# First stage of a spectral filter and bilinear GLU kernel by pairs of row tiles

## The chip, the cores and the metric

The kernel runs on one core of a Trainium2 chip. The metric is device time in microseconds (us) for one execution. Engines are named as in the profile: PE is the matrix engine and PEld its weight loads, DVE the vector engine, ACT the scalar (activation) engine, POOL the GpSimd engine, SP the queue that issues most transfers. Each engine takes its own instructions strictly in program order and waits on semaphores for the others.

## The reference

Two residual layers on an array of 2048 rows and 640 columns, all float32. The change touches only the beginning of the first one.

```python
x = A_x                                            # [1, 2048, 640]
X = rfft2(layernorm(x)) * (w_r + 1j * w_i)         # [2048, 321] spectrum
h = x + irfft2(X, s=(2048, 640))
g, u = layernorm(h) @ w_gate, layernorm(h) @ w_up  # 640 -> 1728
out = h + (g * u) @ w_down                         # 1728 -> 640
```

Layer norm has no weights: each row is shifted by its mean and scaled by the inverse root of its variance plus 1e-5.

## The kernel before

The 2048 rows lie in 16 row tiles of 128. The Fourier transforms are done as matrix products with tables.

**The first stage** (lines 255 to 298) treats one row tile `t` at a time and leaves a partial transform in the array `s1`. What follows, from line 300 on, needs all 16 tiles of `s1`, so the next stage's first matrix product (the helper at line 82, reading `tab` and `s1`) can't begin before tile 15 is in `s1`. For a tile the engines do this:

- Statistics. For tiles 1, 4, 5 and 10 to 15, ACT makes two passes over the row with an accumulated sum (lines 149 and 150, in `moments`; the written rows go to a scratch part of `fold` and aren't used). For the others DVE uses its batch-norm instructions (134 to 136). Tiles form groups for the next step: (0), (1), (2,3), (4,5), (6 to 9), (10 to 13), (14,15). `inverse_root` then needs a square root on ACT (159, result `sd`) and four short DVE steps: a reciprocal (160), then 161, 162 and 163. The work of a group is spread over earlier tiles by the lists `dve` and `acts`. The root of a group goes to `post`, called in the iteration two tiles ahead of the group's first tile; the four DVE steps go to the iteration after it.
- Fold. The row is folded about its middle. POOL writes the differences (`odd`, line 183), DVE writes the sums less twice the mean (193), and then DVE adds the ends of the folded halves (the small sums `j`, 66 numbers a row, line 197) and subtracts them (320 numbers a row, line 198).
- Table. `scale_c` multiplies a constant 128x128 table by the row's inverse root (line 217 on DVE, or 215 on ACT for tile 0), so that the layer norm's scale enters by the matrix product.
- Product. `s1_mm`: six matrix instructions with the folds (line 209). The first four read the folded halves, the last two read `j`; so two thirds can run before lines 197 and 198 are done, the rest not. A seventh (line 210) reads `j` too and goes to a bank of its own. A float32 product counts as two passes in the profile: 12 for line 209 and 2 for line 210.
- Evacuation. ACT copies the tile's result to `s1`: `s1_main` (228, 512 numbers a row) and `s1_rest` (223, 128 numbers a row).

`fold` has four buffers, so tile `t` takes the place of tile `t - 4`. The tables `crs` have four places too. The main result bank has two buffers; the bank for the last product has one for even and one for odd tiles.

What sets the order is the loop at line 265: the order of calls is the order in each engine's queue. In iteration `t` ACT gets `s1_rest(t - 1)`, the statistics of `acts[t]`, the root in `post[t]` and `s1_main(t - 1)`; DVE gets the three fold steps of tile `t`, zipped with the short steps of `dve[t]`, and then the table of tile `t + 1`.

Of the kernel before, what the change touches and what calls it, by code (L numbers as in the profile page):

```python
# [11 lines left out]
F32 = mybir.dt.float32  # L12
F32R = mybir.dt.float32r
AF = mybir.ActivationFunctionType
OP = mybir.AluOpType

P = 128
S, D, NF, FF = 2048, 640, 321, 1728
NT = S // P
# [2 lines left out]
NC = 14  # L22
FW = (160, 193, 161, 161)
FOFF = (0, 160, 353, 514)
NR = 4
ON_ACT = (1, 4, 10, 14)
EPS = 1e-5

# [1 line left out]
def view(t, offset, dims):  # L30
    return bass.AP(tensor=t.tensor, offset=t.offset + offset, ap=[list(t.ap[0])] + [list(d) for d in dims])
# [6 lines left out]
def zipped(main, side):  # L38
    n = len(main)
    for i, f in enumerate(main):  # L40
        f()
        for h in side[i * len(side) // n:(i + 1) * len(side) // n]:
            h()
# [3 lines left out]
def tile_spectral_glu(ctx: ExitStack, tc: tile.TileContext, x, wf, wgu, wlast, wdown, wdlast,  # L47
                      cc, ci, fmain, frem, imain, irem, mm, out):
    nc = tc.nc
# [3 lines left out]
    small = ctx.enter_context(tc.tile_pool(name="small", bufs=4))  # L53
    ctx.enter_context(tc.manual_schedule())

    tt, act = nc.vector.tensor_tensor, nc.scalar.activation
# [9 lines left out]
    def bank(tag, bufs=2):  # L66
        return pools["a"].tile([P, 512], F32, tag=tag, name=tag, bufs=bufs)
# [31 lines left out]
    def home(tag, shape, name, dt=F32):  # L99
        return keep.tile(shape, dt, tag=tag, name=name)  # L100
# [10 lines left out]
    s1r = home("wA", [P, 2, NG, P], "s1r", F32R)  # L111
    fold = home("qm", [P, NR * 1026 + 2 * D], "fold")
    wts = home("wB", [P, 3, 2, 2, NQ], "wts")
# [10 lines left out]
    def moments(ts, junk=None, total=None):  # L124
        n = len(ts)
        m2 = small.tile([P, n], F32, tag="m2", name="m2")
        ve = small.tile([P, n], F32, tag="ve", name="ve")
        if junk is None:
            mv = small.tile([P, n, 2], F32, tag="mv", name="mv")

            def one(t, i):
                st = small.tile([P, 2, 6], F32, tag="st", name="st")
                return [
                    lambda: nc.vector.bn_stats(st[:, 0], X[t][:, 0:320]),
                    lambda: nc.vector.bn_stats(st[:, 1], X[t][:, 320:640]),
                    lambda: nc.vector.bn_aggr(mv[:, i], st),
                ]

            fs = [f for i, t in enumerate(ts) for f in one(t, i)]
            fs.append(lambda: nc.vector.tensor_scalar(m2, mv[:, :, 0], 2.0, None, op0=OP.mult))  # L140
            fs.append(lambda: nc.vector.tensor_scalar(ve, mv[:, :, 1], EPS, None, op0=OP.add))
            return m2, ve, fs
        sq = small.tile([P, n], F32, tag="sq", name="sq")
        fs = []
        if total is not None:
            fs.append(lambda: nc.vector.tensor_scalar(m2, total, 2.0 / D, None, op0=OP.mult))
        for i, t in enumerate(ts):
            if total is None:
                fs.append(lambda t=t, i=i: act(junk[i], X[t], AF.Identity, scale=2.0 / D, accum_out=m2[:, i:i + 1]))  # L149
            fs.append(lambda t=t, i=i: act(junk[i], X[t], AF.Square, bias=m2[:, i:i + 1], scale=-2.0,  # L150
                                           accum_out=sq[:, i:i + 1]))
        fs.append(lambda: nc.vector.tensor_scalar(ve, sq, 0.25 / D, EPS, op0=OP.mult, op1=OP.add))
        return m2, ve, fs
# [14 lines left out]
    def front(ts):  # L168
        n = len(ts)
        r = small.tile([P, n], F32, tag="r", name="r")  # L170
        junk = [fold[:, o:o + D] for o in (NR * 1026, NR * 1026 + D)]
        m2, ve, fs = moments(ts, junk * 2 if ts[0] in ON_ACT else None)
# [4 lines left out]
    def folded(t):  # L177
        o = t % NR * 1026
        return fold[:, o:o + 642], fold[:, o + 642:o + 1026]

    def odd(t):
        f = folded(t)[0]
        nc.gpsimd.tensor_tensor(view(f, 0, [[160, 2], [1, 160]]), view(XP[t], 1, [[320, 2], [1, 160]]),
                                view(XP[t], 639, [[-320, 2], [-1, 160]]), op=OP.subtract)

    def even(t):
        f, j = folded(t)

        def both(n):
            return view(f, 0, [[320, 2], [1, n]]), view(f, 160, [[321, 2], [1, n]])  # L190

        return [
            lambda: nc.vector.scalar_tensor_tensor(view(f, 320, [[161, 2], [1, 161]]),
                                                   view(XP[t], 0, [[320, 2], [1, 161]]), SC[t][1],
                                                   view(XP[t], 640, [[-320, 2], [-1, 161]]),
                                                   op0=OP.subtract, op1=OP.add),
            lambda: tt(view(j, 33, [[-33, 2], [1, 33]]), *both(33), op=OP.add),
            lambda: tt(view(j, 64, [[1, 2], [2, 160]]), *both(160), op=OP.subtract),
        ]

    PS1, CR = {}, {}

    def s1_mm(t):
        pm, pr = PS1[t] = bank("im"), bank("ir2" if t % 2 else "im2", 1)
        (f, j), c = folded(t), CR[t]
        sums = [(f[:, o:o + P], f[:, o + n:o + n + P]) for o, n in ((31, 160), (353, 161))]
        for k, ls in enumerate((*sums, (view(j, 128, [[2, P]]),), (view(j, 129, [[2, P]]),))):
            for n, l in enumerate(ls):
                nc.tensor.matmul(pm[:, k * P:(k + 1) * P], l, c, start=n == 0, stop=n == len(ls) - 1)  # L209
        nc.tensor.matmul(pr[:, 0:P], j[:, 0:P], c, start=True, stop=True)  # L210

    def scale_c(t):
        CR[t] = crs[t % 4]
        if t == 0:
            act(CR[t], cct, AF.Copy, scale=SC[t][0])
        else:
            nc.vector.tensor_scalar(CR[t], cct, SC[t][0], None, op0=OP.mult)

    def at(base, t):
        return view(base, 4 * t, [[64, 32], [1, 4]])  # L220

    def s1_rest(t):
        act(at(s1[:, 4], t), PS1[t][1][:, 0:P].rearrange("p (g m) -> p g m", g=32), AF.Copy)

    def s1_main(t):
        n = 4 if t < NT - 1 else 2
        for c in range(0, 4, n):
            act(view(s1, 4 * t + 2048 * c, [[2048, n], [64, 32], [1, 4]]),
                PS1[t][0][:, c * P:(c + n) * P].rearrange("p (c g m) -> p c g m", c=n, g=32), AF.Copy)
# [6 lines left out]
    dve = [[] for _ in range(NT)]  # L236
    acts = [[] for _ in range(NT)]
    post = {}
# [23 lines left out]
        post[first - 2] = cs[0]  # L262
        dve[first - 1] += cs[1:]
    odd(0)
    for t in range(NT):
        if t == 1:
            nc.gpsimd.dma_start(frt, frem)
        if t >= 1:
            s1_rest(t - 1)
            for f in acts[t]:  # L270
                f()
        if t:
            zipped(even(t), dve[t])
        else:
            e0 = even(0)
            for f in e0[:1] + c0 + e0[1:] + f1:
                f()
        if t >= 1:
            if t in post:
                post[t]()  # L280
            s1_main(t - 1)
        else:
            scale_c(0)
            for f in c1[:1] + acts[0]:
                f()
            zipped(dve[0], c1[1:])
        if t + 1 < NT:
            if t < 2:
                nc.gpsimd.tensor_copy(small.tile([P, 1], F32, tag="hold", name="hold"), folded(t)[1][:, 383:384])
            odd(t + 1)  # L290
            scale_c(t + 1)
        if t == 0:
            post[t]()
        s1_mm(t)
    s1_main(NT - 1)
    s1_rest(NT - 1)
    part(0, nc.vector)
# [743 lines left out]
    for n, (blk, p) in enumerate(steps):  # L1041
        if p == 6:
            s13, s12 = count % 3, (count + 1) % 3
            if blk == 0:
                load_raw(0)
                copies, sums, high, low = prep(0, blk, nc.vector)
# [24 lines left out]
            else:  # L1071
                copies, sums, high, low = prep(0, blk)
# [222 lines left out]
```

## Time and profile before

| what | value |
|---|---|
| median of 3 runs | 707.47 us (707.27 to 707.54) |
| the profiled execution's own time | 707.21 us |
| its span, first to last instruction | 705.2 us |
| what lies around the span | 2.0 us |
| busy share of the span: PE, PEld, DVE, ACT, POOL | 97%, 85%, 68%, 43%, 53% |
| granted clock of PE | 0.999 |
| first stage: first product of tile 0 to last `s1_main` | 8.46 us to 45.82 us |

Shares over the whole span mix stages with different limits. The first stage is 37 us of 705, and there DVE is the busy engine while PE has gaps; after it PE is nearly always busy. So what the change is worth has to be read from the first 46 us alone. In the rows of the timeline the first two numbers are the start and the duration in us, and the bracket at the end holds the idle time before the row and what ended it. Consecutive instructions of a kind are merged into one row (x12).

### The profile page before, as it was taken

How to read it: one execution, taken by the hardware profiler on the slowest of the kernel's cores; microseconds unless marked ns; L12 is line 12 of the kernel's file. 1: busy time of each engine (PE TensorE's matmuls, PEld its weight loads, DVE VectorE, ACT ScalarE, POOL GpSimd, SP SyncE). 2: the span in 40 equal slices, each digit the busy share in tenths (PEclk: the TensorE clock that was granted, in tenths of full speed). 3: DMA queues.
4: the chain of work that ended last, by engine and by line, in shares of the span. 5: the costliest groups of instructions: out<-in, count | busy, mean ns of one | idle time of the engine just before them, and what ended most of it. 6: DMA issues, size and time to landing. Idle time of an engine off the chain costs nothing.

```text
span 705.2 us, 10146 instructions
## 1 busy us (share of the span) xinstructions
PE 685.1 (97%) x3784; PEld 602.7 (85%) x3784; DVE 476.1 (68%) x830; ACT 305.3 (43%) x586; POOL 374.4 (53%) x355
## 2 busy tenths in 40 slices
PE   7899998999989999999999999999999999999998
PEld 6798997977878898988888889888888988888887
DVE  7968887798968445656565659555665656565654
ACT  4856776355543323242523355353333342424320
POOL 3312224332144586877868643148596877867610
PEclk9999999999999999999999999999999999999999
DMA  9405665002321211203020262311211103030203
GB/s 335 182 8 194 224 212 173 1 19 94 113 76 37 75 39 34 78 1 113 0 86 28 94 221 97 132 38 37 76 38 45 68 5 109 0 105 9 74 1 150
DMA packets 23233, 60.30 MB, mean 86 GB/s; under 512 B 2576, under 2 KB 7184, under 8 KB 23184
## 3 DMA queue, kind: packets, MB, share of 16 engines
q1 hardware_dynamic: 22608, 57.94, 23.9%
q0 software_dynamic: 288, 1.48, 0.6%
q8 instruction: 30, 0.49, 0.3%
q10 hardware_dynamic: 288, 0.23, 0.1%
q14 instruction: 19, 0.16, 0.1%
HBM read 51.78 MB, written 7.86 MB: 85 GB/s over the span
## 4 chain that ended last, share of the span: by engine, by line
PE 81%; DVE 10%; issue 5%; ACT 3%; DMA 1%; POOL 0%; SPq 0%; DVEq 0%; POOLq 0%; ACTq 0%
PE e L82 43%; PE y L82 25%; PE re L82 2%; PE im L82 2%; PE u L342 2%; PE eo L82 2%; PE im L209 1%; DVE ex L752 1%; PE im L392 1%; PE im L391 1%; PE ir L383 1%; DMA raw<-in_wgu_dram 1%; DVE x L515 1%; ACT fold L149 1%; DMA x<-in_x_dram 1%
## 5 line engine op out<-in xcount | busy, mean ns | idle before, releaser
L82 PE MATMUL e<-xt,wst 128*128 128x512 f32 x864 | 219.0, 392 | 1.7 <-ACT u L661 1.7
L82 PEld LDWEIGHTS e<-xt,wst 128*128 128x128 f32 x864 | 158.0, 188 | 29.1 <-ACT u L661 2.1
L82 PE MATMUL y<-wd,ht 128*128 128x320 f32 x880 | 150.8, 310 | 1.3 <-DVE x L513 1.0
L82 PEld LDWEIGHTS y<-wd,ht 128*128 128x128 f32 x880 | 138.7, 188 | 13.1 <-DVE x L513 1.3
L716 POOL TENSOR_TENSOR wst<-raw,wst 128x1024 fp32r<-128x1024 f32 x24 | 57.7, 2403 | 91.2 <-ACT wst L715 91.1
L82 PE MATMUL e<-t,wst 128*128 128x512 f32 x288 | 74.1, 391 | 0.0
L732 POOL TENSOR_TENSOR wst<-raw,wst 128x896 fp32r<-128x896 f32 (+1 forms) x46 | 65.1, 1438 | 8.0 <-ACT wst L727 8.0
L926 DVE TENSOR_TENSOR xb<-y,xb 128x640 f32<-128x640 f32 x60 | 49.5, 824 | 26.0 <-PE y L82 24.5
L748 ACT ACTIVATE ht<-e 128x512 fp32r<-128x512 f32 x48 | 27.6, 596 | 88.2 <-DVE rawh L844 44.4
L82 PEld LDWEIGHTS e<-t,wst 128*128 128x128 f32 x288 | 52.6, 188 | 8.5
L926 DVE TENSOR_TENSOR x<-y,x 128x640 f32<-128x640 f32 x48 | 39.5, 824 | 20.8 <-PE y L82 19.3
L1011 DVE TENSOR_TENSOR m<-e,m 128x512 f32<-128x512 f32 x24 | 16.5, 687 | 46.5 <-PE e L82 46.4
L752 DVE TENSOR_TENSOR ht<-e,ht 128x512 fp32r<-128x512 f32 x48 | 33.1, 689 | 17.6 <-ACT ht L748 17.0
L727 ACT ACTIVATE wst<-raw 128x896 fp32r<-128x896 f32 (+1 forms) x48 | 30.1, 677 | 31.5 <-POOL raw L721 30.7
L82 PE MATMUL y<-ex,ht 128*128 128x320 f32 x216 | 43.5, 309 | 0.0
L469 POOL TENSOR_TENSOR wd<-draw,wd 128x640 fp32r<-128x640 f32 x10 | 16.4, 1660 | 50.0 <-ACT wd L468 50.0
L82 PE MATMUL e<-xt,wdir 128*128 128x512 f32 x180 | 42.1, 393 | 0.0
L82 PEld LDWEIGHTS e<-xt,wdir 128*128 128x128 f32 x180 | 33.5, 188 | 7.2 <-issue 0.2
L82 PEld LDWEIGHTS y<-ex,ht 128*128 128x128 f32 x216 | 36.2, 188 | 3.1
L882 ACT ACTIVATE wd<-draw 128x640 fp32r<-128x640 f32 x18 | 13.3, 740 | 58.7 <-POOL draw L895 48.1
L82 PE MATMUL e<-ht,wst 128*128 128x512 f32 x144 | 38.4, 392 | 0.0
L513 DVE TENSOR_TENSOR x<-y,x 128x640 f32<-128x640 f32 x32 | 26.2, 819 | 17.7 <-PE y L82 17.7
(214 smaller groups left out, 1293.4 us busy)
## 6 DMA issues: line engine op xcount, KB each, us to landing
raw<-in_wgu_dram SPq DMA_DIRECT2D x24, 640.0 KB, 4.0
wts<-in_wf_dram SPq DMA_DIRECT2D x16, 644.0 KB, 4.3
draw<-in_wdown_dram SPq DMA_DIRECT2D x24, 320.0 KB, 4.5
x<-in_x_dram SPq DMA_DIRECT2D x16, 320.5 KB, 6.1
bits<-in_mm_dram SPq DMA_DIRECT2D x32, 128.0 KB, 3.9
sp<-x SPq DMA_DIRECT2D x8, 320.0 KB, 2.2
xb<-sp SPq DMA_DIRECT2D x8, 320.0 KB, 5.7
out_dram<-x SPq DMA_DIRECT2D x8, 320.0 KB, 2.3
```

Source lines behind the costliest of these rows:

```text
L82: nc.tensor.matmul(o, l, r, start=start, stop=stop, skip_group_check=True)
L342: nc.tensor.matmul(ps[h][:, 0:NQ], WM[g][0][:, h], T[g][:, h], start=True, stop=True)
L469: los.append(lambda r=r, a=a, b=b: engine.tensor_tensor(w[:, 1, a:b], r, f32(w[:, 0, a:b]), op=OP.subtract))
L513: tt(xv, ps[:, :, 0:320], xv, op=OP.add)
L716: nc.gpsimd.tensor_tensor(wa[:, 1], stage[:, 0:1024], f32(wa[:, 0]), op=OP.subtract)
L727: act(ws[:, 0, o:o + b - a], stage[:, a:b], AF.Copy)
L732: ptt(ws[:, 1, o:o + b - a], stage[:, a:b], f32(ws[:, 0, o:o + b - a]), op=OP.subtract)
L748: act(unit(u)[0], src, AF.Copy)
L752: engine.tensor_tensor(lo, src, f32(hi), op=OP.subtract)
L882: act(w[:, 0, a:b], r, AF.Copy)
L926: tt(xv, PQ[q][:, :, 0:320], xv, op=OP.add)
L1011: tt(m5, acc_a, m5, op=OP.add)
```

## The change

From tile 2 on, tiles are taken in pairs `(t, t + 1)`.

- The sums less twice the mean stay one DVE instruction a tile (`sum_fold`, now line 202). The small sums of both tiles become one DVE instruction (line 196), and so do the differences (line 197). They therefore come after the sums of both tiles.
- `fold` has six buffers instead of four.
- The tables of tiles 4 to 15 are made by ACT (line 221) instead of DVE (line 223).
- The loop is written anew. At the head of the iteration of a pair, ACT gets `s1_main` and `s1_rest` of both tiles of the pair before; then `acts[t]`, `post[t]`, `acts[t + 1]` and the tables of the next pair.
- Tiles 0 and 1 keep their order, except that `s1_main(0)` follows at once on tile 1's fold and `odd(3)` and `scale_c(3)` come ahead of pair (2,3).

Later lines have moved: 193 is 202, 197 is 196, 198 is 197, 209 is 215, 210 is 216, 217 is 223, 215 is 221, 223 is 229, 228 is 234. Lines 134 to 183 keep their numbers.

```diff
-NR = 4
+NR = 6
@@ even
+    def even(t, n=1):
+        def twice(v, o, dims):
+            return view(v, o, ([[1026, n]] if n > 1 else []) + dims)
+        def both(w):
+            f = folded(t)[0]
+            return twice(f, 0, [[320, 2], [1, w]]), twice(f, 160, [[321, 2], [1, w]])
+        j = folded(t)[1]
+        return [sum_fold(t + k) for k in range(n)] + [
+            lambda: tt(twice(j, 33, [[-33, 2], [1, 33]]), *both(33), op=OP.add),
+            lambda: tt(twice(j, 64, [[1, 2], [2, 160]]), *both(160), op=OP.subtract),
+        ]
@@ scale_c
-        if t == 0:
+        if t == 0 or t >= 4:
             act(CR[t], cct, AF.Copy, scale=SC[t][0])
@@ the loop
+    odd(3)
+    scale_c(3)
+    for t in range(2, NT, 2):
+        for p in range(max(1, t - 2), t):
+            s1_main(p)
+            s1_rest(p)
+        for f in acts[t]:
+            f()
+        sums = even(t, 2)
+        zipped(sums[:1], dve[t])
+        if t in post:
+            post[t]()
+        for f in acts[t + 1]:
+            f()
+        zipped(sums[1:], dve[t + 1])
+        if t + 2 < NT:
+            for n in range(t + 2, t + 4):
+                odd(n)
+                scale_c(n)
+        s1_mm(t)
+        s1_mm(t + 1)
+    s1_main(NT - 2)
+    s1_rest(NT - 2)
+    s1_main(NT - 1)
+    s1_rest(NT - 1)
```

**ACT around the root of the group of tiles 6 to 9** (`sd_175`). Before, the evacuations of tile 2 (`im_272`) and tile 3 (its rest `ir2_297`) stand ahead of it, and tile 3's main part (`im_296`) behind it:

```order
L228 ACTIVATE s1_82<-im_272 128x128x4
L223 ACTIVATE s1_82<-ir2_297 128x32x4
L149 ACTIVATE fold_84,m2_178<-x1_67 128x640
L150 ACTIVATE fold_84,sq_180<-x1_67,m2_178 128x640
L159 ACTIVATE sd_175<-ve_169 128x4
L228 ACTIVATE s1_82<-im_296 128x128x4
```

Now, with tile 3's results named `im_294` and `ir2_295`, and tile 4's `im_327`:

```order
L229 ACTIVATE s1_82<-im2_286 128x32x4
L234 ACTIVATE s1_82<-im_294 128x128x4
L229 ACTIVATE s1_82<-ir2_295 128x32x4
L149 ACTIVATE fold_84,m2_178<-x1_67 128x640
L150 ACTIVATE fold_84,sq_180<-x1_67,m2_178 128x640
L159 ACTIVATE sd_175<-ve_169 128x4
L149 ACTIVATE fold_84,m2_178<-x1_67 128x640
L150 ACTIVATE fold_84,sq_180<-x1_67,m2_178 128x640
L221 ACTIVATE bits_86<-cct_78,r_167 128x128 x2
L234 ACTIVATE s1_82<-im_327 128x128x4
```

Tile 3's main part has moved ahead of the root; two tables stand between the statistics and the next evacuation.

**DVE at the same place**, tiles 4 and 5. Before, tile 4's folds (two `TENSOR_TENSOR` rows) are ahead of the reciprocal that reads the root, and only tile 5's are behind it:

```order
L193 SCALAR_TENSOR_TENSOR fold_84<-x0_66,m2_162 128x322
L136 BN_AGGR mv_170<-st_174 128x2
L197 TENSOR_TENSOR fold_84<-fold_84 128x2x33
L140 TENSOR_SCALAR m2_168<-mv_170 128x4
L198 TENSOR_TENSOR fold_84<-fold_84 128x2x160
L141 TENSOR_SCALAR ve_169<-mv_170 128x4
L217 TENSOR_SCALAR bits_86<-cct_78,r_161 128x128
L193 SCALAR_TENSOR_TENSOR fold_84<-x0_66,m2_162 128x322
L160 RECIPROCAL r_167<-sd_175 128x4
L197 TENSOR_TENSOR fold_84<-fold_84 128x2x33
L161 SCALAR_TENSOR_TENSOR w_176<-r_167 128x4
L198 TENSOR_TENSOR fold_84<-fold_84 128x2x160
```

Now:

```order
L202 SCALAR_TENSOR_TENSOR fold_84<-x0_66,m2_162 128x322
L136 BN_AGGR mv_170<-st_174 128x2
L140 TENSOR_SCALAR m2_168<-mv_170 128x4
L141 TENSOR_SCALAR ve_169<-mv_170 128x4
L202 SCALAR_TENSOR_TENSOR fold_84<-x0_66,m2_162 128x322
L160 RECIPROCAL r_167<-sd_175 128x4
L196 TENSOR_TENSOR fold_84<-fold_84 128x2x2x33
L161 SCALAR_TENSOR_TENSOR w_176<-r_167 128x4
L197 TENSOR_TENSOR fold_84<-fold_84 128x2x2x160
```

The small sums and the differences of tile 4 have moved behind the reciprocal, into the instructions of the pair.

**ACT around the root of tiles 10 to 13** (`sd_181`). Before, with tile 7's main part `im_376` and tile 6's `im_358`:

```order
L228 ACTIVATE s1_82<-im_358 128x128x4
L223 ACTIVATE s1_82<-ir2_377 128x32x4
L149 ACTIVATE fold_84,m2_184<-x1_67 128x640
L159 ACTIVATE sd_181<-ve_179 128x4
L228 ACTIVATE s1_82<-im_376 128x128x4
```

Now, with tiles 6 and 7 named `im_361` and `im_370`:

```order
L150 ACTIVATE fold_84,sq_180<-x1_67,m2_178 128x640
L149 ACTIVATE fold_84,m2_178<-x1_67 128x640
L150 ACTIVATE fold_84,sq_180<-x1_67,m2_178 128x640
L221 ACTIVATE bits_86<-cct_78,r_167 128x128 x2
L234 ACTIVATE s1_82<-im_361 128x128x4
L229 ACTIVATE s1_82<-im2_362 128x32x4
L234 ACTIVATE s1_82<-im_370 128x128x4
L229 ACTIVATE s1_82<-ir2_371 128x32x4
L149 ACTIVATE fold_84,m2_184<-x1_67 128x640
L159 ACTIVATE sd_181<-ve_179 128x4
```

Two tables and the four evacuations of a whole pair have moved between the statistics and this root. The root of tiles 14 and 15 likewise stands behind the four evacuations of tiles 10 and 11.

More of the change, by code (lines that the diff above doesn't have):

```diff
@@ L184, in odd, with sum_fold @@
                                 view(XP[t], 639, [[-320, 2], [-1, 160]]), op=OP.subtract)
[L186 to L193, printed above, removed]
+    def even(t, n=1):
[9 more added lines that the diff above has]
+        ]
+    def sum_fold(t):
+        f = folded(t)[0]
+        return lambda: nc.vector.scalar_tensor_tensor(view(f, 320, [[161, 2], [1, 161]]),
                                                    view(XP[t], 0, [[320, 2], [1, 161]]), SC[t][1],
                                                    view(XP[t], 640, [[-320, 2], [-1, 161]]),
[L196 to L199, printed above, removed]
+                                                   op0=OP.subtract, op1=OP.add)
     PS1, CR = {}, {}
@@ L264, in tile_spectral_glu @@
     odd(0)
-    for t in range(NT):
-        if t == 1:
+    for t in range(2):
+        if t:
             nc.gpsimd.dma_start(frt, frem)
-        if t >= 1:
-            s1_rest(t - 1)
-            for f in acts[t]:
-                f()
-        if t:
-            zipped(even(t), dve[t])
+            s1_rest(0)
+            for f in acts[1]:
+                f()
+            zipped(even(1), dve[1])
+            s1_main(0)
         else:
@@ L277, in tile_spectral_glu @@
                 f()
[L278 to L282, printed above, removed]
             scale_c(0)
@@ L286, in tile_spectral_glu @@
             zipped(dve[0], c1[1:])
[L287 to L291, printed above, removed]
-        if t == 0:
-            post[t]()
+        nc.gpsimd.tensor_copy(small.tile([P, 1], F32, tag="hold", name="hold"), folded(t)[1][:, 383:384])
+        odd(t + 1)
+        scale_c(t + 1)
+        if t == 0:
+            post[0]()
+        s1_mm(t)
[10 more added lines that the diff above has]
+        if t in post:
+            post[t]()
+        for f in acts[t + 1]:
[5 more added lines that the diff above has]
+                scale_c(n)
         s1_mm(t)
+        s1_mm(t + 1)
+    s1_main(NT - 2)
+    s1_rest(NT - 2)
     s1_main(NT - 1)
```

## The prediction

> **What bounds the kernel now.** I looked first at the engines' busy time and clock by stretch, then at the timeline of the first 46 us, engine by engine.
>
> ```profile
> 8.00:20.00 12.00, 7.58 (x52) 6.19 (x50) 11.69 (x43) 6.31 (x19) 5.98 (x9) 1.00 1.06 402
> 60.00:110.00 50.00, 50.00 (x339) 46.31 (x338) 41.96 (x57) 35.05 (x89) 13.85 (x35) 1.00 0.67 217
> ```
>
> After the length, the columns are PE, PEld, DVE, ACT and POOL busy time, then the clock, DMA share and GB/s. Up to 20 us DVE is busy 11.69 of 12.00 us and PE 7.58. Right after the first stage PE is busy 50.00 of 50.00 us: what the stage loses or gains passes on whole, and nothing there waits for an absolute time. The bandwidth row, 40 slices of the first 60 us, says the same of the transfers:
>
> ```profile
> GB/s 0 114 313 398 400 409 397 403 404 403 392 406 401 381 414 380 375 78 11 0 0 0 0 0 11 0 0 0 0 0 0 0 0 0 59 29 124 345 69 244
> ```
>
> Nearly nothing moves between 27 and 50 us; all that the stage needs has arrived.
>
> I mark tile n by T(n), the start of its last weight load (line 210; sixteen such rows in tile order):
>
> ```profile
> 13.42 0.30 PEld L210 LDWEIGHTS ir<-bits,fold 128*128 128x128 f32 x2
> 20.51 0.30 PEld L210 LDWEIGHTS ir<-bits,fold 128*128 128x128 f32 x2
> 25.00 0.30 PEld L210 LDWEIGHTS ir<-bits,fold 128*128 128x128 f32 x2
> 33.54 0.30 PEld L210 LDWEIGHTS ir<-bits,fold 128*128 128x128 f32 x2
> 35.35 0.55 PEld L209 LDWEIGHTS im<-bits,fold 128*128 128x128 f32 x4 [0.26 <-DVE fold L198]
> 35.83 0.30 PEld L210 LDWEIGHTS im<-bits,fold 128*128 128x128 f32 x2
> 36.05 0.97 PEld L209 LDWEIGHTS im<-bits,fold 128*128 128x128 f32 x8
> 37.81 0.30 PEld L210 LDWEIGHTS ir<-bits,fold 128*128 128x128 f32 x2
> 40.04 1.44 PEld L209 LDWEIGHTS im<-bits,fold 128*128 128x128 f32 x12
> 41.40 0.30 PEld L210 LDWEIGHTS ir<-bits,fold 128*128 128x128 f32 x2
> 41.62 0.97 PEld L209 LDWEIGHTS im<-bits,fold 128*128 128x128 f32 x8
> 44.86 0.30 PEld L210 LDWEIGHTS ir<-bits,fold 128*128 128x128 f32 x2
> 45.16 0.66 ACT L228 ACTIVATE s<-im 128x256 f32<-128x256 f32 x2 [0.60 <-PE im L209]
> ```
>
> So T(1) = 13.42, T(3) = 20.51, T(5) = 25.00, T(9) = 33.54, T(11) = 37.81, T(13) = 41.40, T(15) = 44.86; the stage's last evacuation starts at T(15) + 0.30. A tile without waits takes PE 1.58 us (40.04 to 41.62), of which 1.36 lead up to T. From the third part, which reads `j`, to the next tile it is 0.70 (35.35 to 36.05). That part waits for DVE's line 198.
>
> **What one tile costs on DVE and ACT.**
>
> ```profile
> 42.65 0.28 DVE L217 TENSOR_SCALAR bits<-cct,r 128x128 f32<-128x128 f32 x1
> 42.85 0.55 DVE L193 SCALAR_TENSOR_TENSOR fold<-x,m 128x322 f32<-128x322 f32 x1
> 43.50 0.23 DVE L197 TENSOR_TENSOR fold<-fold 128x66 f32<-128x66 f32 x1
> 43.76 0.49 DVE L198 TENSOR_TENSOR fold<-fold 128x320 f32<-128x320 f32 x1
> 28.26 0.74 ACT L149 ACTIVATE fold<-x 128x640 f32<-128x640 f32 x1
> 29.12 0.83 ACT L150 ACTIVATE fold<-x,m 128x640 f32<-128x640 f32 x1
> 29.95 0.57 ACT L228 ACTIVATE s<-im 128x512 f32<-128x512 f32 x1
> 30.58 0.73 ACT L149 ACTIVATE fold<-x 128x640 f32<-128x640 f32 x1
> 31.30 0.19 ACT L159 ACTIVATE sd<-ve 128x4 f32<-128x4 f32 x1
> ```
>
> DVE: table 0.20 to the next start, sums 0.65, small sums 0.26, and about 0.40 for the differences, whose last 0.09 overlap: 1.51 us a tile alone. ACT: full statistics 1.69 (28.26 to 29.95), evacuation 0.63, so 2.32 us for a tile with both. POOL's fold holds up DVE besides:
>
> ```profile
> 22.61 1.22 POOL L183 TENSOR_TENSOR fold<-x 128x320 f32<-128x320 f32 x1 [1.64 <-DVE ve L141]
> 22.90 0.19 ACT L159 ACTIVATE sd<-ve 128x4 f32<-128x4 f32 x1
> 23.12 0.18 DVE L160 RECIPROCAL r<-sd 128x4 f32<-128x4 f32 x1
> 23.21 0.70 DVE L197 TENSOR_TENSOR fold<-fold 128x66 f32<-128x66 f32 x1
> 23.95 0.49 DVE L198 TENSOR_TENSOR fold<-fold 128x320 f32<-128x320 f32 x1
> 33.14 0.75 POOL L183 TENSOR_TENSOR fold<-x 128x320 f32<-128x320 f32 x1 [0.84 <-DVE w L162]
> ```
>
> Line 197 takes 0.70 instead of 0.23 and ends at 23.91, just behind POOL's 23.83: it waited. A fold costs POOL 0.75 alone. The same rows show the root (0.22 from its start to the reciprocal's), then 0.09 to the next DVE instruction.
>
> **The change, part by part.** *Longer instructions.* From 66 to 320 numbers lines 197 and 198 go from 0.23 to 0.49, so 1.04 ns a number. Twice 66 is then 0.30 and twice 320 is 0.82; fixed cost paid twice would give 0.46 and 0.98, the other bound. I take the first, since a row of nearly that size shows it:
>
> ```profile
> L348 DVE TENSOR_TENSOR y<-u,wts 128x644 f32<-128x644 f32 x14 | 11.6, 829 | 1.9 <-PE u L342 1.6
> L215 ACT ACTIVATE bits<-cct,r 128x128 f32<-128x128 f32 x1 | 0.4, 386 | 0.0
> ```
>
> A pair saves DVE 0.26 + 0.40 - 0.07 - 0.33 = 0.26 us in these, and 0.40 for its two tables: 0.66 of 3.02. Twelve tables go to ACT at 0.39 each, 0.30 to the next start if they overlap by 0.09 as lines 149 to 228 do; bounds 0.2 to 0.39. The Trainium skill ("ScalarE: Activation LUTs", What ACT_TABLE_LOAD costs) would make it 280 + 0.833 x 128 = 387 ns, which the row bears out; its rules for kernel authors put a multiplication on VectorE, not ScalarE, and by them twelve tables would add 12 x 0.39 = 4.7 us of ACT time to save 12 x 0.28 = 3.4 of DVE. Where ACT sets the pace this works against the change; in the sum below only two tables do.
>
> *The new wait.* A group's reciprocal stands on DVE between the sums of tile t + 1 and the pair's small sums. Its root on ACT now stands behind the evacuation of tile t - 1, which waits for PE to finish that tile. Behind the waiting reciprocal are the small sums and differences of both tiles, and for these PE waits with the third part of tile t. It is a closed round: PE, ACT, DVE, PE. Before, tile t's folds were already through, and the root did not wait for tile t - 1's main part.
>
> From the reciprocal on, a round costs 0.09 + (0.30 + 0.03) + 0.82 + 0.05 (from the end of 198 at 16.88, in the rows below, to PE at 16.93) + 0.70 + 1.36 = 3.35 to T(t + 1); I call this F. To evacuate a tile takes 0.30 + 0.63 after its T.
>
> - Tiles 2, 3. Their DVE work changes by +0.07 + 0.33 - 0.13 - 0.55 = -0.28, the last two being the small sums and differences of tile 2 from these rows:
>
> ```profile
> 15.71 0.21 DVE L197 TENSOR_TENSOR fold<-fold 128x66 f32<-128x66 f32 x1
> 15.84 0.48 DVE L135 BATCH_NORM_STATS2 st<-x 128x6 f32<-128x320 f32 x1
> 16.25 0.63 DVE L198 TENSOR_TENSOR fold<-fold 128x320 f32<-128x320 f32 x1
> 16.80 0.20 DVE L136 BATCH_NORM_AGGREGATE mv<-st 128x2 f32<-128x12 f32 x1
> 16.93 0.55 PEld L209 LDWEIGHTS im<-bits,fold 128*128 128x128 f32 x4 [1.30 <-DVE fold L198]
> ```
>
>   With six buffers POOL runs two more folds here in a row, at 0 to 0.75 us; I take 0.2. Tile 3's differences ended at 19.98 (T(3) less 0.48, 35.35 to 35.83, less 0.05); the pair's end at 19.9 to 20.0, but PE then still has the rest of tile 2 and all of tile 3: T(3) = 20.0 + 0.05 + 0.70 + 1.36 = 22.1, **+1.6** (+1.2 to +2.2).
> - Tiles 4, 5. Evacuate tile 3, full statistics, root: T(5) - T(3) = 0.93 + 1.69 + 0.22 + F = 6.2 against 4.49, **+1.7** (+1.5 to +1.9).
> - Tiles 6 to 9. ACT: evacuate 5, two statistics, two tables (0.60), evacuate 6 and 7 (1.26), line 149 and root, 30.58 to 31.30 before, so 0.72, root 0.22: 0.93 + 3.38 + 0.60 + 1.26 + 0.72 + 0.22 + F = 10.5 against 8.54, **+1.9** (+1.6 to +2.2, mostly by the tables).
> - Tiles 10, 11. No root. DVE alone needs 2.4 from differences to differences (0.66 less than 3.02), with POOL's two folds up to 3.9; PE needs 3.16. I take 3.6 against 4.27, **-0.7** (-1.1 to -0.4).
> - Tiles 12, 13. Evacuate 11, root: 0.93 + 0.22 + F = 4.5 against 3.59, **+0.9** (+0.7 to +1.1).
> - Tiles 14, 15. DVE has its work done by then; PE 2 x 1.58 = 3.16 against 3.46, **-0.3**.
>
> Sum: 1.6 + 1.7 + 1.9 - 0.7 + 0.9 - 0.3 = **+5.1 us**, bounds +3.6 to +6.6. Behind the stage no instruction is added or moved. The profiled execution took 707.21 us with a span of 705.2; its counterpart would take 712.3. The median lies 0.26 higher, so **712.5 us**.
>
> **The rivals.**
>
> *The waits don't bite and the saving shows* (6%). If the roots came early enough, as at 22.90 before, pairs would run at DVE's or PE's pace. From T(3) at 22.1, six pairs at 3.6 end at 43.7 instead of 44.86: 1.2 us faster, 706.3; at PE's 3.16 each, 703.7. For it: 23.12 shows the reciprocal with hardly a wait. Against it: the queue order on ACT.
>
> *PE's clock drops in the new gaps* (10%). PE would sit idle about 4 us ahead of tile 2's third part and 3 us ahead of tile 4's. If its passes then ran at half speed, the 2.06 us of PE work in F would double in these two rounds: +2 to +4, 714.5 to 716.5. For it: passes just after the start took 320 ns against 287 in the stage. Against it: granted clock 1.00 in every stretch, with PE busy only 7.58 of 12.00 us. The Trainium skill ("TensorE: Matmul & The Clock Gate", Part 1) states the rule: the clock halves after an idle window of about 3.4 us. Before, the longest gap within the stage is 1.3 us (16.93), so no run here shows it.
>
> ```profile
> L250 PE MATMUL re<-warm 128*128 128x128 f32 x48 | 7.1, 320 | 1.1 <-DVE warm L247 1.1
> L209 PE MATMUL im<-bits,fold 128*128 128x128 f32 x192 | 27.7, 287 | 6.8 <-DVE fold L198 2.5 <-DVE bits L217 1.3 <-POOL fold L183 0.9
> ```
>
> *The pair instructions save nothing* (5%): at 0.46 and 0.98 the five rounds that pass through them grow by 0.32 each, 714.1. The row of 644 numbers speaks against it.
>
> *A later stage absorbs it* (3%): 707.5. The 50.00 of 50.00 speaks against it.
>
> **How the numbers follow.** The forecast has 76%; 712.5 is its time, with 711.0 to 714.0 from the bounds of the sum. To hold the time 8 times in 10 the range goes a little beyond, 710.0 to 715.2, and takes in the rivals on the slow side in part. A difference of 0.2%, 1.4 us, is about what a measurement can tell from no change. Slower: forecast, clock and pair rivals, 91%. Same: absorption and most of the milder half of the first rival, 4%. Faster: its other half, 5%.
>
> **What would show it.** Right: idle time ahead of line 160 on DVE ended by ACT's root, 2 to 3 us in the rounds of tiles 4 and 8 and about 1 us at 12; gaps of PE ended by line 197; T(15) near 50 us; pair instructions of 0.30 and 0.82 us. Wrong: T(15) below 46, roots that finish ahead of tile t - 1's evacuation, or a busy PE between 60 and 110 us that starts as early as before. A granted clock below 0.99 would show the clock rival.

## The result, and the profile after

The changed kernel takes **718.41 us** (median, 717.44 to 719.00) against 707.50 of the kernel before, measured beside it: a ratio of 1.0149 (95% interval 1.0133 to 1.0164). It is slower, as forecast, but by 10.9 us and not by 5.1, and lies above the range. The profiled execution has a span of 716.6 us against 705.2.

Nearly all of it is lost in the first stage. The tile marks of the forecast, T(n), are now these rows of PE's weight loads (start, duration; line 216 was 210):

```profile
13.67 0.30 PEld L216 LDWEIGHTS ir<-bits,fold 128*128 128x128 f32 x2
24.31 0.51 PEld L216 LDWEIGHTS ir<-bits,fold 128*128 128x128 f32 x2
32.04 0.30 PEld L216 LDWEIGHTS ir<-bits,fold 128*128 128x128 f32 x2
44.30 0.54 PEld L216 LDWEIGHTS ir<-bits,fold 128*128 128x128 f32 x2
47.93 0.30 PEld L216 LDWEIGHTS ir<-bits,fold 128*128 128x128 f32 x2
52.57 0.30 PEld L216 LDWEIGHTS ir<-bits,fold 128*128 128x128 f32 x2
55.75 0.30 PEld L216 LDWEIGHTS ir<-bits,fold 128*128 128x128 f32 x2
```

They are tiles 1, 3, 5, 9, 11, 13 and 15 (the rows between are left out). T(15) is 55.75 instead of 44.86, 10.9 us later, of the 11.4 us between the two spans; no run settles the other 0.5. Behind the stage PE is as busy as it was from 60 to 110 us before (columns as in the prediction):

```profile
71.00:121.00 50.00, 50.00 (x339) 46.30 (x338) 41.96 (x57) 34.94 (x89) 13.79 (x36) 1.00 0.67 216
```

The predicted wait is there. DVE's reciprocals (the last figure is the idle time ahead, and what ended it):

```profile
18.51 0.15 DVE L160 RECIPROCAL r<-sd 128x2 f32<-128x2 f32 x1
27.32 0.18 DVE L160 RECIPROCAL r<-sd 128x4 f32<-128x4 f32 x1 [4.57 <-ACT sd L159]
39.18 0.18 DVE L160 RECIPROCAL r<-sd 128x4 f32<-128x4 f32 x1 [2.06 <-ACT sd L159]
49.19 0.17 DVE L160 RECIPROCAL r<-sd 128x2 f32<-128x2 f32 x1 [1.34 <-ACT sd L159]
```

The first row, in the pair of tiles 2 and 3, has no wait; the gap of 3.83 us ahead of tile 2's third part, the longest one below, therefore does not come from a wait for the root. It is ended by the pair's differences, which stand behind the sums of both tiles. Of the later gaps, those ended by line 197 (2.89, 1.76 and 1.18 us) follow from the wait; the one of 2.11 us stands ahead of tile 8's first part, and in PE's rows an evacuation by ACT ends it (at 37.66 us, 1.95 us idle, line 234). Behind the gaps many passes take longer. PE's weight loads in the first pairs, and in the last ones for comparison:

```profile
20.51 0.93 PEld L215 LDWEIGHTS im<-bits,fold 128*128 128x128 f32 x4 [3.83 <-DVE fold L197]
...
21.75 2.68 PEld L215 LDWEIGHTS im<-bits,fold 128*128 128x128 f32 x12
...
28.61 0.93 PEld L215 LDWEIGHTS im<-bits,fold 128*128 128x128 f32 x4 [2.89 <-DVE fold L197]
...
37.63 1.11 PEld L215 LDWEIGHTS im<-bits,fold 128*128 128x128 f32 x8 [2.11 <-issue]
40.50 0.93 PEld L215 LDWEIGHTS im<-bits,fold 128*128 128x128 f32 x4 [1.76 <-DVE fold L197]
...
41.74 2.68 PEld L215 LDWEIGHTS im<-bits,fold 128*128 128x128 f32 x12
...
50.51 0.55 PEld L215 LDWEIGHTS im<-bits,fold 128*128 128x128 f32 x4 [1.18 <-DVE fold L197]
...
54.38 1.45 PEld L215 LDWEIGHTS im<-bits,fold 128*128 128x128 f32 x12
```

Twelve passes take 2.68 us instead of 1.45, four 0.93 instead of 0.55. The reason stands in the stretches of the span. The granted clock changes at 17.92, 24.74, 28.16, 31.57, 38.40 and 45.22 us, all of them on one grid of 3.41 us, and the stretches below are cut on that grid. The columns after the length are PE's busy time, the granted clock, the DMA share and GB/s:

```profile
14.51:17.92 3.41, 1.37 (x8) 1.00 1.05 400
17.92:21.33 3.41, 0.82 (x4) 0.50 1.05 393
21.33:24.74 3.41, 3.41 (x18) 0.50 1.05 397
24.74:28.16 3.42, 1.17 (x10) 1.00 0.29 111
28.16:31.57 3.41, 2.96 (x14) 0.50 0.02 5
31.57:34.98 3.41, 3.41 (x32) 1.00 0.01 2
34.98:38.40 3.42, 1.48 (x13) 1.00 0.00 0
38.40:41.81 3.41, 1.95 (x10) 0.50 0.00 0
41.81:45.22 3.41, 3.41 (x18) 0.50 0.00 0
45.22:48.64 3.42, 3.42 (x30) 1.00 0.00 0
48.64:52.05 3.41, 2.42 (x21) 1.00 0.00 0
```

Read each row with the next: after a stretch in which PE was busy for 1.37, 0.82, 1.17, 1.48 or 1.95 us the next one has half the clock; after 2.42 us and more it has the full one. So the clock was half for five stretches, 17.1 us. PE was busy for 0.82 + 3.41 + 2.96 + 1.95 + 3.41 = 12.6 us of that; twelve passes take 1.45 us at full clock instead of 2.68, so an estimated 12.6 x (1 - 1.45 / 2.68) = 5.8 us of PE's time is at stake, less what the next gap hides.

The Trainium skill ("TensorE: Matmul & The Clock Gate", Part 1) describes a free-running window of 3413 ns, which the trace bears out to 0.01 us. It puts the fall of the clock after an idle window; here the windows ahead of a fall held up to 1.48 us of passes, so the measurement asks for less idleness than that.

### The profile page after: what moved, and what is told of

Its sections match the earlier page's. It is cut to its first block, busy times and chain, and to the rows that moved or that the text cites. A ratio compares the mean times of both kernels' runs of the same rounds, so it can differ in the third digit from the quotient of the medians.

```text
span 716.6 us, 10107 instructions
## 1 busy us (share of the span) xinstructions
PE 689.2 (96%) x3784; PEld 607.7 (85%) x3784; DVE 471.4 (66%) x804; ACT 309.2 (43%) x598; POOL 373.8 (52%) x355
## 3 DMA queue, kind: packets, MB, share of 16 engines
q0 software_dynamic: 288, 1.48, 0.6%
## 4 chain that ended last, share of the span: by engine, by line
PE 80%; DVE 10%; issue 5%; ACT 3%; DMA 1%; POOL 0%; SPq 0%; DVEq 0%; POOLq 0%; ACTq 0%
PE e L82 42%; PE y L82 24%; PE re L82 2%; PE im L82 2%; PE im L215 2%; PE u L363 2%; PE eo L82 2%; DVE ex L773 1%; PE im L413 1%; PE im L412 1%; PE ir L404 1%; DVE x L536 1%; DVE x L534 1%; DMA raw<-in_wgu_dram 1%; ACT fold L149 1%
## 5 line engine op out<-in xcount | busy, mean ns | idle before, releaser
L947 DVE TENSOR_TENSOR x<-y,x 128x640 f32<-128x640 f32 x48 | 39.6, 824 | 20.8 <-PE y L82 19.9
L215 PE MATMUL im<-bits,fold 128*128 128x128 f32 x192 | 31.5, 318 | 14.1 <-DVE fold L197 9.5
L215 PEld LDWEIGHTS im<-bits,fold 128*128 128x128 f32 x192 | 28.4, 227 | 16.1 <-DVE fold L197 10.6
```

The source lines that it names most:

```text
L947: tt(xv, PQ[q][:, :, 0:320], xv, op=OP.add)
```

## Experiments

Theory A: the forecast's wait opens the gaps, and the gaps halve PE's clock. Against it stand: the waits alone (B, the half clock lies in time that PE would have waited anyway); another cause of the clock (C); the pair instructions, the tables on ScalarE or the six buffers by themselves (D to J, each named with its run). Each experiment shows its edit against the kernel named.

### e1: PE kept busy in the gaps (changed kernel)

```diff
+FILL = {2: (0, 12), 4: (0, 10), 8: (6, 5), 12: (0, 3)}
 for k, ls in enumerate(...):            # in s1_mm
+    if k in (0, 2):
+        for _ in range(FILL.get(t, (0, 0))[k // 2]):
+            nc.tensor.matmul(pw[:, 0:P], warm, warm, start=True, stop=True)
```

> The changed kernel with matmuls of the zero tile `warm` in PE's gaps: 12 ahead of tile 2's third part, 10 ahead of tile 4's, 6 and 5 ahead of tile 8's first and third part, 3 ahead of tile 12's. All real work and its order are kept; the filler takes about 0.29 us a matmul and fits the gaps of 3.83, 2.89, 2.11, 1.76 and 1.18 us. Theory A, the waits alone would have cost the forecast +5.1 and PE's clock, which fell in the gaps, the other +5.3 to +5.8: the granted clock stays 1.00, twelve passes take 1.45 us again instead of 2.68, the last weight load of tile 15 starts near 50.5 us instead of 55.75, time 712.5 to 713.5. Rival B, the half rate only marks time that PE would have waited for DVE and ACT anyway: the clock stays up, but tile 15 stays near 55 us and the time near 718. Rival C, the clock is lowered by something other than idle time of PE (the transfers, the start): it still shows 0.5, time 718 or more.

712.98 us (ratio 1.0081, 1.0063 to 1.0100), as A has it. Matmuls that compute nothing make the kernel 5.4 us faster. In the profiled execution the clock was half in one stretch of this stage, 16.00 to 19.41 us, while PE ran filler, and in a later one (see e9); it took 715.19 us, and the three others, at a clock of 1.000, 712.72 to 713.07. The tile marks (lines moved by four):

```profile
13.51 0.30 PEld L220 LDWEIGHTS ir<-bits,fold 128*128 128x128 f32 x2
22.80 0.30 PEld L220 LDWEIGHTS ir<-bits,fold 128*128 128x128 f32 x2
29.03 0.30 PEld L220 LDWEIGHTS ir<-bits,fold 128*128 128x128 f32 x2
39.55 0.30 PEld L220 LDWEIGHTS ir<-bits,fold 128*128 128x128 f32 x2
43.09 0.30 PEld L220 LDWEIGHTS ir<-bits,fold 128*128 128x128 f32 x2
47.68 0.30 PEld L220 LDWEIGHTS ir<-bits,fold 128*128 128x128 f32 x2
50.87 0.30 PEld L220 LDWEIGHTS ir<-bits,fold 128*128 128x128 f32 x2
```

At half clock the twelve fillers ahead of tile 2's third part run too long:

```profile
16.82 4.00 PEld L217 LDWEIGHTS re<-warm 128*128 128x128 f32 x24
19.50 0.81 DVE L198 TENSOR_TENSOR fold<-fold 128x640 f32<-128x640 f32 x1
20.74 0.56 PEld L219 LDWEIGHTS im<-bits,fold 128*128 128x128 f32 x4
```

The pair's differences (198 here) end at 20.31, and the third part starts at 20.74 instead of 0.05 us behind them, as it does in the changed kernel. So 0.38 us of the first term below is the filler's own; the clock did not slow the other terms.

Differences of these marks, less the same differences before, give the forecast's terms in e1 and, from the rows further above, in the changed kernel:

| tiles | forecast | e1 (less filler) | changed kernel |
|---|---|---|---|
| 2, 3 | +1.6 (1.2 to 2.2) | +2.20 (+1.82) | +3.55 |
| 4, 5 | +1.7 | +1.74 | +3.24 |
| 6 to 9 | +1.9 | +1.98 | +3.72 |
| 10, 11 | -0.7 | -0.73 | -0.64 |
| 12, 13 | +0.9 | +1.00 | +1.05 |
| 14, 15 | -0.3 | -0.27 | -0.28 |
| sum | +5.1 | +5.9 (+5.5) | +10.6 |

Where the clock was up in both, the last three terms agree; where it fell, the changed kernel has 1.73 + 1.50 + 1.74 = 5.0 us on top. B and C fall.

### e2 and e3: the wait taken out, on DVE or on ACT (changed kernel)

```diff
 e2:
-        zipped(sums[1:], dve[t + 1])
+        for f in sums[1:] + dve[t + 1]:
+            f()
 e3:
-        for p in range(max(1, t - 2), t):
-            s1_main(p)
-            s1_rest(p)
-        for f in acts[t]:
-            f()
         sums = even(t, 2)
...
-        for f in acts[t + 1]:
+        for p in range(max(1, t - 2), t):
+            s1_main(p)
+            s1_rest(p)
+        for f in acts[t] + acts[t + 1]:
             f()
```

> The changed kernel with one thing moved on DVE: the reciprocal and the other instructions of the next group (root's steps, and on the early pairs statistics) stand behind the pair's small sums and differences instead of among them; ACT's order, pair instructions, six buffers and tables by ScalarE as changed. Theory A, the closed round PE, ACT, DVE, PE is what opened the gaps, and the gaps are what lowered the clock: the differences no longer wait for the root, no reciprocal holds up the pair's folds, the longest gap of PE falls below 2 us, the clock falls at most once, and at least 7 of the 10.9 us come back: 708.5 to 711.5, tile 15 near 47 to 49 us. Rival D, the pair instructions or the tables on ScalarE themselves make the gaps (DVE's and POOL's or ACT's pace): gaps of 3 us remain, time 716 to 719.

> The changed kernel with one thing moved on ACT: the statistics and the root of a group stand ahead of the four evacuations of the pair before, not behind them; DVE's order as changed. Theory A: the root no longer waits for PE, the reciprocal hardly waits on DVE (idle ahead of line 160 under 0.7 us instead of 4.57, 2.06 and 1.34), the evacuations come later and may hold up PE by its result banks; tile 15 near 48 to 50 us, clock down at most once, 709.5 to 712.5. Rival D, as in the run before, pair instructions and tables set the pace: 716 to 719. Rival E, the evacuations that are pushed back stall PE as much as the root did: the gaps of PE stand ahead of a tile's first part, ended by ACT, time 714 or more.

e2: 710.49 us (1.0039, 1.0026 to 1.0052); T(15) = 47.82; one fall of the clock in this stage, after a stretch with 0.38 us of passes ahead of tile 2's third part. The longest gap is still 3.22 us there, above the 2 us expected, so most of this gap is not the root's; behind it none exceeds 2. e3: 711.12 us (1.0052, 1.0036 to 1.0068); T(15) = 49.81; no reciprocal waits, but the clock fell twice (15.35 to 25.6 us, 35.8 to 39.2 us), once more than expected. The gap ahead of tile 2's third part is still 3.43 us here too. What remains of the gaps behind it stands ahead of a tile's first part and is ended by ACT's evacuations, by rows of PE:

```profile
29.82 1.61 PE L215 MATMUL im<-bits,fold 128*128 128x128 f32 x12 [1.35 <-ACT s L234]
35.14 2.28 PE L215 MATMUL im<-bits,fold 128*128 128x128 f32 x12 [1.90 <-ACT s L234]
```

That is rival E's place, at a smaller price. Either edit breaks the closed round, and 7 to 8 of the 10.9 us come back with pairs, tables and buffers left as changed. D falls, as far as these 7 us go.

### e5 and e6: parts of the change undone, the wait kept (changed kernel)

```diff
 e5, in even():
-            lambda: tt(twice(j, 33, ...), *both(33), op=OP.add),
-            lambda: tt(twice(j, 64, ...), *both(160), op=OP.subtract),
+        [f for k in range(n) for f in one(k)]    # both instructions for tile t, then for t + 1
 e6:
-        if t == 0 or t >= 4:
+        if t == 0:
             act(CR[t], cct, AF.Copy, scale=SC[t][0])
```

> The changed kernel with the pair instructions undone, their place in the order kept: small sums and differences of the two tiles by two instructions of 66 and two of 320 numbers, in the same stretch behind the sums of the second tile; the reciprocal of the next group still stands ahead of them. Theory A, the order is what costs, not the length of the instructions: about 0.2 us more of DVE a pair, PE begins tile t about 0.4 us earlier and then waits for tile t + 1; the clock still falls two or three times; 716.5 to 720. Rival F, PE waits because both tiles' folds end together in one instruction: gaps a good deal shorter, 714 or less.

e5: 714.42 us (1.0082, 1.0059 to 1.0106), below A's 716.5 and just above F's 714. With single instructions tile t's differences are ready earlier, and PE's gaps shrink: 2.42 us ahead of tile 2's third part instead of 3.83, 2.28 instead of 2.89 ahead of tile 4's. The clock fell for three stretches instead of five (15.66 to 22.48 and 36.1 to 39.6 us), and in one execution hardly at all: 711.04 us at a clock of 0.998. That one against e1's 712.72 to 713.07 at 1.000 puts the pairing itself at some 2 us, by one execution alone. So pairing the instructions seems to cost something here: tile t has to wait for tile t + 1's share. My expectation had that as cancelled by the wait for the next tile.

> The changed kernel with the tables of tiles 4 to 15 by VectorE again, as in the kernel before (0.28 us each on DVE instead of about 0.34 on ACT). By the forecast's sum only the round of tiles 6 to 9 has tables on ACT's path (0.60 us), and DVE has room ahead of the others: theory A gives 0.6 us less to 0.6 us more, and the clock, which falls by the same gaps, keeps its 5 us: 717 to 719.5. Rival G, the tables on ScalarE carry the loss (they hold up statistics and roots): at least 4 us come back, 714 or less.

e6: 715.79 us (1.0120, 1.0105 to 1.0136), 1.2 below A's range and above G's 714. In the profile T(15) is 55.26, and the clock falls three times at the same places (17.94, 28.2 and 38.4 us). The round of tiles 6 to 9 takes 11.65 instead of 12.26 us, which is the 0.60 of the two tables; tiles 10 and 11 give back 0.38 of it; T(15) - T(1) is 41.91 against 42.08. So the tables do not carry the loss. The median moved by more than the marks; the other executions show a clock of 0.990 to 0.995 against 0.988 to 0.990 of the changed kernel, and two lows fewer would make such a difference, but no run settles it.

### e7: the three parts without the wait, with filler in the gaps

e2's edit and e1's filler, 12, 3 and 6 matmuls ahead of tile 2's, tile 4's and tile 8's parts.

> The kernel with the reciprocal behind the pair's folds on DVE (run with that edit: 710.5, one fall of the clock, at tile 2) and filler matmuls in the gaps ahead of tile 2's third part (12), tile 4's (3) and tile 8's first (6). It has the three parts of the change without its wait and without the clock's fall. Theory A: the low stretch there cost PE at most half of 3.4 us, 1.7: tile 15 at 46.1 to 47.0 us, 708.5 to 710.0, so still not faster than before, since the gap of 3.2 us ahead of tile 2 and 2.0 ahead of tile 8 stay as idle time. Rival H, the three parts by themselves save DVE and so time, once wait and clock are out of the way: below 706.5.

710.20 us (1.0039, 1.0026 to 1.0053), 0.2 above A's range; T(15) = 46.99. From T(3) to T(15) it takes 46.99 - 22.55 = 24.44 us, against 24.35 before: from tile 4 on, pairs, tables and buffers neither gain nor lose. From T(1) to T(3) it takes 9.08 against 7.09, and there lies the rest, 2.0 us. Not all of it is the change's: the clock was half here from 15.49 to 18.91 us, and the fillers hold up tile 2's third part until 20.48, 0.8 us after the pair's differences end (18.84 + 0.83 = 19.67):

```profile
16.78 3.78 PEld L217 LDWEIGHTS re<-warm 128*128 128x128 f32 x24
18.84 0.83 DVE L198 TENSOR_TENSOR fold<-fold 128x640 f32<-128x640 f32 x1
20.48 0.56 PEld L219 LDWEIGHTS im<-bits,fold 128*128 128x128 f32 x4
```

About 1.2 us are left: PE still gets tiles 2 and 3 together and late. H falls even with 0.8 us taken off: no gain below 706.5 was hidden under the wait.

### e11 and e12: parts of the change alone (kernel before)

```diff
 e11:
-        if t == 0:
+        if t == 0 or t >= 4:
             act(CR[t], cct, AF.Copy, scale=SC[t][0])
 e12:
-NR = 4
+NR = 6
```

> The kernel before with one part of the change alone: the tables of tiles 4 to 15 by ScalarE; single tiles, four buffers. Theory: from tile 10 on it gives the 0.6 us of the run with tiles 10 to 15 alone; in tiles 4 to 9, where ScalarE has statistics and evacuations of 2.32 us a tile, four tables add 0.3 to 0.4 each, up to 1.4 us: 707.0 to 708.4. Rival G, the tables carry the loss: 710 or more.

> The kernel before with one part of the change alone: six fold buffers instead of four. POOL can run two folds further ahead, which come down on DVE's instructions (line 197 took 0.70 instead of 0.23 beside a fold): 707.0 to 708.2. Rival J, the folds that POOL runs ahead hold DVE up by several us: 710 or more.

e11: 708.61 us (1.0011, 1.0000 to 1.0022), 0.2 above the range expected. T(9) - T(3) is 35.20 - 20.85 = 14.35 against 13.03, so +1.3 over tiles 4 to 9, where ACT has statistics besides; T(15) - T(9) is 10.68 against 11.32, -0.6. e12: 707.60 us (1.0001, 0.9992 to 1.0011): no difference. Both profiled executions also lost the clock in the first stage, e11 from 17.37 to 20.79 us and e12 from 17.43 to 24.26, after windows with 1.78 and 1.93 us of passes; e12's T(15) is 45.57 there, 0.7 later than before. So single tiles, too, can lose the clock at this place. Neither part alone is worth more than about a microsecond; G and J fall.

### e4 and e8: tables by ScalarE only where it has room (kernel before)

```diff
 e4:
-        if t == 0:
+        if t == 0 or t >= 10:
 e8, beside that:
+FILL = {1: (2, 2), 2: (0, 4), 3: (0, 2)}     # filler as in e1
```

> The kernel before with one part of the change alone, for tiles 10 to 15 only: their tables by ScalarE (six instructions of 0.28 us leave DVE, six of about 0.39 us go to ACT); single tiles, four buffers. Theory: from tile 10 on DVE has no statistics and ACT none but the last group's, ACT has room, and PE waits there for line 198 and line 217 by 0.2 to 0.3 us a tile: up to 0.6 us less, 706.9 to 707.4, at the edge of what can be told. Rival, the waits for POOL's folds and ACT's evacuations set this stretch: 707.3 to 708.0.

> The kernel before with the tables of tiles 10 to 15 by ScalarE (run: 706.5) and filler matmuls in the gaps of tiles 1 to 3 (2 and 2, 4, 2), where PE is busy for under 2.0 of 3.4 us. Theory A, the clock goes by PE's busy share in stretches of 3.41 us whose grid is not tied to the kernel's start, so that the kernel before loses it too in the executions whose grid lies badly (707.5 to 709.1 of its runs, clock 0.995 to 0.997): no run above 707, clock 1.00 in all, median 706.1 to 706.5. Rival I, those runs are slower for another reason: the spread of 2 us stays, median 706.5 or more by the filler.

e4: 706.54 us, a ratio of 0.9988 (0.9979 to 0.9997), 0.4 below the range expected; T(15) = 44.41 instead of 44.86. e8: 706.26 us (0.9986, 0.9977 to 0.9995), but three of eleven executions took 707.1 to 707.9. The filler in the first stage did not take the spread away, so A's expectation missed: the place was wrong, as the next run shows. The execution with 707.10 kept a clock of 1.000; what made it slower no run shows.

### e9 and e10: filler where the clock is lost by chance

Four profiles of experiments (e1, e2, e5, e7) show one more stretch at half clock, which begins between 124.7 and 128.6 us; e11's and e12's, run beside e9, have it at 123.2. In the others there is none. In the kernel before, this place is at 118.5 to 122 us, ahead of line 82's first product onto `eo`. In e2's profile the stretch ahead of the fall and the one after it read:

```profile
122.28:125.70 3.42, 1.77 (x13) 1.46 (x12) 1.56 (x4) 1.34 (x3) 1.50 (x5) 1.00 0.00 0
125.70:129.10 3.40, 3.40 (x15) 3.40 (x14) 0.45 (x2) 0.44 (x1) 0.55 (x3) 0.50 0.00 0
```

PE is busy for 1.77 of 3.42 us there (PE, PEld, DVE, ACT, POOL, then the clock). In the profile of before the same place also has 1.76 of 3.40 us from 118.54 on, yet no fall. Its grid lies otherwise: the trace's one fall is at 703.93 us, behind the last product, and 171 steps of 3.4133 us (e5's edges at 15.66 and 128.30 us are 33 of them apart) back from there lies an edge at 120.25 us. The two windows beside this edge hold 2.24 and 2.11 us of passes. In e4 and e8, counted back in the same way, one window there holds 1.77 us and the clock stays up, so the share alone does not settle it. e9 puts five matmuls into the 1.30 us gap:

```diff
     for g in (NG - 2, NG - 1):
         is2_mm(g)
         is2_out(g)
+    pw = bank("re")
+    for n in range(5):
+        nc.tensor.matmul(pw[:, 0:P], cct, cct, start=True, stop=True)
```

> The kernel before with five filler matmuls in the 1.30 us gap ahead of the stage that starts at 122 us (line 82 onto `eo`), nothing else. In four profiles of experiments the clock was low for one stretch right there, after a stretch in which PE was busy for 1.77 of 3.41 us, and in the others it was not; of the 34 unprofiled runs of the kernel before about a third lie 1.5 to 2 us above the rest at a clock of 0.995 to 0.997. Theory A (the grid of 3.41 us falls otherwise in each execution, and PE at half rate for one stretch costs 3.41/2 = 1.7 us where PE is the bound): no or hardly any runs above 708, clock 0.998 to 1.00, mean lower by about 0.5 us, median 706.9 to 707.2. Rival I, those runs are slower for another reason: a third of the runs stays at 708.4 to 709.

> The kernel before with the tables of tiles 10 to 15 by ScalarE, filler in the gaps of tiles 1 to 3 and the five fillers ahead of the stage at 122 us: the version that should be faster than both. Theory A: 706.0 to 706.4, no run above 707.5. Rival I: median the same, single runs at 707.5 to 708.2 as with the tables alone.

e9's profile has, in the same place:

```profile
118.54:121.94 3.40, 2.87 (x22) 1.00 0.00 0
```

Of e9's eleven executions none took more than 707.87 us; of the 33 of the kernel before, measured beside it, 13 took 708.06 to 708.97, at clocks of 0.995 to 0.998. The mean falls from 707.73 to 707.27; the medians (707.32 and 707.37) do not tell, 0.9992 (0.9983 to 1.0001), and e9's is 0.1 above what was expected. The step of some 1.7 us, half of 3.41, is what one stretch at half clock costs where PE sets the pace. Rival I, which would have kept a third of the runs up there, falls.

e10, with all of it: **706.39 us, a ratio of 0.9983 (0.9974 to 0.9992)**, one of eleven executions above 706.8 (708.06), where A expected none above 707.5. It beats both kernels, by 1.0 and 12.0 us of their medians (707.37 measured beside it, 718.41 earlier).

## Why the prediction was wrong in size

*Direction and mechanism held.* The reciprocal's wait, its cause in ACT's order, the closed round and its length were right; tile 4's wait is 4.57 us in the changed kernel and 3.08 in e1, where 2 to 3 were forecast. With the clock up the kernel takes 712.7 to 713.1 us, against the forecast's 712.5. Five of six terms came within 0.1.

*Tiles 2 and 3* were short by 0.2 with the clock up. The forecast had the pair's differences end at 19.9 to 20.0 us and gave 0.2 of a possible 0.75 to POOL's two further folds; in the changed kernel the differences end at 20.46:

```profile
13.36 4.88 POOL L183 TENSOR_TENSOR fold<-x 128x320 f32<-128x320 f32 x6
19.65 0.81 DVE L197 TENSOR_TENSOR fold<-fold 128x640 f32<-128x640 f32 x1
```

Six folds in a row last until 18.24 us. Of this half microsecond 0.25 lies already in T(1), 13.67 instead of 13.42. By the forecast's own steps T(3) - T(1) is 20.46 + 0.05 + 0.70 + 1.36 - 13.67 = 8.90 us against 7.09, +1.8, as in e1 without the filler's share. The bound (2.2) held that.

*The step that failed* is the one where the gaps met the clock. The forecast worked out gaps of about 4 and 3 us (3.83 and 2.89 measured), priced a fall of the clock, and then left it out of the sum as a rival of 10%. Its ground against the fall, clock 1.00 with PE busy for 7.58 of 12.00 us, was a mean of 63% over a long stretch. What counts is the share in each 3.41 us. In the fourteen profiles, from 8.5 us on, every window at full clock with less than 1.7 us of passes (50%) was followed by half the clock, and none with more than 2.0 us (58%) was. Between these, busy time alone doesn't decide: e3 lost the clock after 1.93 us and e2 after 1.77 (shown at e9), while e5 kept it after 1.72:

```profile
11.94:15.35 3.41, 1.93 (x13) 1.00 1.08 405
```

```profile
22.48:25.89 3.41, 1.72 (x15) 1.00 0.94 355
25.89:29.31 3.42, 2.75 (x22) 1.00 0.04 12
```

The kernel before ran just above that band (2.11 and 2.21 us in its windows from 14.44 and 17.85 us), so that gaps of 2 to 4 us brought it below. By the rule cited from the Trainium skill ("TensorE: Matmul & The Clock Gate", Part 1), an idle window of about 3.4 us, tile 4's gap of 2.89 us would have been spared; the trace shows a fall there as well.

*The rival's price was also too low.* It had two rounds and +2 to +4 us. A third fall came in the round of tiles 6 to 9, from two gaps of 2.11 and 1.76 us with some passes between them. And the half clock holds from one edge of the grid to another, not until PE has work again: from 38.40 us on it lasted two stretches, since the first of them, in which PE waited 1.46 us for DVE, did not bring the clock back. At half clock, windows with up to 2.71 us of passes (e12, from 17.43 us) were followed by half again, and those with 2.94 us (e7, from 15.49 us) and more by the full clock. Measured, the falls cost 718.4 less 712.9, 5.5 us.

*The other rivals.* The row of 0.81 to 0.83 us for 640 numbers and 0.28 to 0.30 for 132 kept the price taken for the pair instructions; nothing was absorbed later; "the waits don't bite" fell with the second row of line 160.

## What to carry to other kernels

When a change opens gaps in PE's work, don't price the gap alone: put PE's busy time in each window of 3.41 us beside the shares at which this kernel kept its clock (always above 58%, never below 50%), and where a window comes below, add half a window for each one that follows with work in it. A filler of a few empty matmuls in the gap is a cheap test of it, and sometimes a gain; one that outlasts the gap costs time itself (0.4 us in e1, 0.8 in e7). And before two tiles are joined into one instruction, look at what stands between them in the queue: the join makes the first tile wait for everything that the second one waits for.

## What was not expected of the hardware

- PE's clock is decided on a grid of 3.41 us that isn't tied to the kernel's start: its edge lay at 14.51 us in the changed kernel, 16.00 in e1, 16.47 in e2 and 15.35 in e3. The same kernel so loses or keeps 1.7 us from one execution to the next: 13 of 33 executions of the kernel before, none of 11 with five empty matmuls at the right place.
- No idle stretch is needed: the clock fell after windows in which PE was busy for up to 57% of the time (1.93 of 3.41 us, e3).
- At half clock a group of twelve passes takes 2.68 us against 1.45, a factor of 1.85.
